# A new order table for a linear-attention and gated-MLP kernel

## The chip, the cores and the metric

The kernel runs on 1 core of one Trainium2 chip. The metric is device time of one execution in microseconds (us). The engines are PE (TensorE), DVE (VectorE), ACT (ScalarE), POOL (GpSimd) and SP (SyncE, which here only issues DMAs).

## The reference, cut to what matters

```python
# attention: 4 batches, 8 heads, 768 steps, head size 48
for t in range(S):
    state = alpha[:, :, t, :, None] * state + einsum('bhd,bhe->bhde', k[:, :, t], v[:, :, t])
    y[:, :, t] = einsum('bhd,bhde->bhe', q[:, :, t], state)
x = y.transpose(0, 2, 1, 3).reshape(B, S, H * D)          # 4 x 768 x 384
h = maximum(x @ w_in, 0)                                    # 384 -> 1024
u, v = h[..., :512], h[..., 512:]
v_n = (v - mean(v)) / sqrt(var(v) + 1e-6)                   # over the 512
v_s = einsum('ts,bsd->btd', w_spatial, v_n) + b_spatial[None, :, None]
out = (u * v_s) @ w_out                                     # 512 -> 384
```

All inputs and the output are float32; the matmuls work on bfloat16 copies.

## The kernel before, in words

**The work.** The recurrence is cut into chunks of 128 steps: 6 chunks a batch, 24 in all, numbered i = 0 to 23. Chunks 0 to 7 are done in pairs j = 0 to 3 (`pair`, even and odd steps in two halves, par 0 and 1); from chunk 8 on one at a time (`first`). A chunk goes through: load of alpha, k, q and v (`ac`, `kc`, `qc`, `vc`); logarithm (`lnp`, `ln`); its running sum as a matmul with a triangle (`cump`, `cum`); two exponentials (`einvp`, `eexpp`); scaled k and q (`ktp`, `qtp`); their transposes (`tr` for pairs, `trk` for single chunks) with copies out of PSUM (`ev`); scores (`sc`) and their mask (`m`); the state's update on PE (`updq`, `upd`) with `z`, `S` and `sb` behind it (`sb` writes the state as the right-hand matrix of the next chunk); the outputs (`ya` for both chunks of a pair, `y` for the part from the state); the copy `xs`, the transposes `xt` and their copies `xe`, which give the MLP its input.

The MLP of batch b then has: `v` (one matmul group a 128-row tile) with its statistics `bn`, `rs` and the normalised `vn`; `u`; `s` (times the spatial matrix, in two parts, mm 0 and mm 1); the product `g`; `o` and the store `st`. The weights are loaded in six pieces: `w_in` half 1, half 0, `w_sp` 0 to 2 and `w_out`, each with copies to bfloat16 (`cast`); the spatial matrix is transposed on PE (`wt`, copies `we`); `bb` and `be` spread its bias.

**The order.** The functions do not emit instructions; they record operations (`Op`) with their engines and dependences in a list. `replay` then goes through the text `PLAN` (lines 57 to 109 of the file) and emits them in that order. A word is an engine's letter (P, D, A, G for POOL, S for the issue of a DMA, Q for its landing) and the operation's number. Each engine runs its own words strictly in the order in which they stand, and an instruction that waits holds up all behind it on that engine. The framework adds the semaphores.

**Fillers.** A number behind a colon, as in `P58:512:512:192`, is a filler: `bank` (line 176) emits an fp32 matmul of so many columns on the constant `junk` (line 188) ahead of the operation, into the PSUM bank that the operation is about to use. The result is never read. Each shows as two matmul records in the trace.

**PSUM.** Eight banks are handed out in turn (`bank`), so an operation that takes a bank also waits for the readers of the bank taken eight turns earlier.

**Tiles of TensorE.** Most matmuls use the full array of 128 rows. The scores, the `trk` and `wt` transposes, the `xt` of single chunks, `ya` and most of `updq` have operands on 64 rows or fewer and use 64-row tiles (`sc` of pairs also 64 columns); `bb` has a single row and uses a 32-row tile. `updq` begins with eight 128-row matmuls (line 536) and goes on with 64-row ones (line 544).

Numbers that the text uses: 49, 51, 53, 55 are the loads of pair 0 (`ac`, `kc`, `qc`, `vc`), 109, 111, 113, 115 those of pair 1; 57 is `lnp,0`, 117 `lnp,1`, 58 `cump,0,0`, 22 `cast,w_in,1,1`, 82 `sb,0`, 96 `y,1`, 94 `xt,0`, 98 `xt,1`, 100 `v,0,0`, 92 `ya,0`, 250 `wt,2`, 259 `wt,5`, 398 `trk,8`, 369 `y,7`.

Lines: 432 and 637 issue the loads of pairs and of single chunks, 1084 those of weights, 443 is `lnp`, 452 `cump`, 502 `tr`, 574 `sc` of pairs, 601 `ya`, 614 `y` of pairs, 365 and 389 `xt`, 710 `trk`, 745 `sc` of single chunks, 831 `wt`; line 819 is the helper through which all MLP matmuls go, 198 and 200 the copies on ACT and on the other engines.

Of the kernel before, what the change touches and what calls it, by code (L numbers as in the profile page):

```python
# [63 lines left out]
G85 P193 A139 P103 D140 S324 Q325 A202 D206 G141 D196 P152 A104 D143 G142 A194 P215 S29 Q30 D105 G192 P153 A330 P157  # L64
G144 P207 D154 A106 G145 D158 P155 P331 D209 A156 D216 P341 A208 P159 G28 A332 D217 P212 A160 G210 A26 D214 P172 G211
A342 D213 P161 A333 G27 A173 D335 P218 S33 Q34 A343 A162 S328 Q329 P219 D345 P170 G334 A220 S382 Q383 D163 P223 P349
P221 A224 S384 Q385 P164 G344 D350 A222 P339 D174 A171 P225 P337 A165 P168 D340 A226 P166 D107 A175 D338 P227 A167
D176 D108 A169 P230 D32 A228 D177 P238 A231 D31 P247 S386 Q387 D35 A239 P347 D232 A248 P250 P244 A249 P242 G36 D229
A348 P236 A252 D251 P362 A233 S37 Q38 G346 D245 P253 D246 A243 G336 P240 D364 A237 S424 Q425 P351 A390 D363 A255 S428
Q429 D235 P359 A254 D234 P391 A352 D353 S388 Q389 P274 D360 A393 A241 G354 P270 A392 D356 P275 D361 A395 G394 P266  # L70
D276 P267 G357 D396 P271 A40 G39 D268 P398 D272 P259 S426 Q427 G355 A400 P365 D399 A261 D260 P256 G358 P405 S430 Q431
D366 A432 P369 P278 G269 D370 S495 Q496 P367 P433 D258 A368 P371 G273 D257 P279 S41 Q42 D407 A372 P294 A434 G397 D406
# [12 lines left out]
P679 S747 Q748 G647 D650 P721 A624 P556 G547 A723 D651 P557 A681 D722 G563 P652 D680 S783 Q784 P682 D558 A653 P686
G555 P728 D683 S877 Q878 P654 D687 P536 A656 G684 A655 P537 D688 A720 S873 Q874 G648 P786 D729 P752 A787 P564 S907
Q908 G685 D538 A754 A758 P724 P657 D730 A753 S875 Q876 G539 A789 P565 D725 A658 D790 S990 Q991 P731 G755 A756 D566
P689 A732 P568 D757 G788 A690 D659 P759 A569 P733 S879 Q880 G726 P691 P576 D734 A692 G559 D625 A735 A760 S909 Q910
P762 P736 A761 G567 D693 D577 S944 Q945 A881 P792 D763 P766 G727 A794 D793 P882 S1027 Q1028 P694 D768 A737 G791 A883
D767 P699 G764 S986 Q987 A884 A695 P795 G765 P769 A886 S950 Q951 D796 P588 A700 G885 A915 D887 S948 Q949 P584 A770  # L90
D797 A696 S946 Q947 P889 D585 P771 A738 P798 D772 P701 A773 D891 A589 D799 P774 A890 D888 S911 Q912 D739 P703 A775
D702 P800 P896 S578 Q579 A704 D801 P580 A660 D802 D898 S304 Q305 P813 A581 D897 S988 Q989 P892 A740 P803 D776 S1023
Q1024 A952 P811 A994 S913 Q914 D661 P697 A814 D742 A804 P916 D741 P572 D893 S300 Q301 A917 D662 A918 P809 D805 G919
A920 S992 Q993 P815 A698 D812 A806 P953 S312 Q313 P829 A955 A573 D808 S590 Q591 P821 D807 A954 S1025 Q1026 D921 P995
A810 P822 G956 A997 S1029 Q1030 A996 P817 A957 D823 G894 S1057 Q1058 P899 A999 P825 D816 G959 A900 P830 D1000 G824
A922 S582 Q583 P818 D958 D831 P826 G998 D819 P901 P923 P960 A903 D827 S1059 Q1060 A925 P837 D902 G828 D820 A962 P926
# [12 lines left out]
"""


# [1048 lines left out]
```

## Time and profile before

| what | value |
|---|---|
| median of 3 runs | 142.24 us (142.18 to 142.88) |
| the profiled execution | 142.43 us |
| its span | 140.6 us |
| PE busy | 135.3 us, 96% of the span |
| DVE, ACT, POOL busy | 118.5, 108.1, 83.9 us |
| mean granted TensorE clock | 0.997 |
| HBM read, written | 23.60 MB, 4.72 MB |

The span runs from the first to the last instruction that the profile shows; the rest of the time lies around it. A busy PE is not PE at its peak: matmuls overlap and their ends are modelled, so the distance from one start to the next is the better measure of what a matmul costs.

### The profile page before, as it was taken

How to read it: one execution, taken by the hardware profiler on the slowest of the kernel's cores; microseconds unless marked ns; L12 is line 12 of the kernel's file. 1: busy time of each engine (PE TensorE's matmuls, PEld its weight loads, DVE VectorE, ACT ScalarE, POOL GpSimd, SP SyncE). 2: the span in 40 equal slices, each digit the busy share in tenths (PEclk: the TensorE clock that was granted, in tenths of full speed). 3: DMA queues.
4: the chain of work that ended last, by engine and by line, in shares of the span. 5: the costliest groups of instructions: out<-in, count | busy, mean ns of one | idle time of the engine just before them, and what ended most of it. 6: DMA issues, size and time to landing. Idle time of an engine off the chain costs nothing.

```text
span 140.6 us, 4974 instructions
## 1 busy us (share of the span) xinstructions
PE 135.3 (96%) x1921; PEld 84.1 (60%) x1921; DVE 118.5 (84%) x292; ACT 108.1 (77%) x279; POOL 83.9 (60%) x148
## 2 busy tenths in 40 slices
PE   7999999999999999999999999999999999999990
PEld 3357566574767656665665765656657666566560
DVE  7187799989999789899689999999899899987850
ACT  3487898899976678999989699989967978751021
POOL 6816458861469996970289999402788599002520
PEclk9999999999999999999999999999999999999998
DMA  4999997989999979989999998999999120005535
GB/s 101 320 324 328 338 254 245 295 286 315 267 226 161 306 145 215 203 175 210 188 199 190 188 200 171 199 200 220 257 222 225 71 107 7 0 23 212 215 146 192
DMA packets 89000, 28.64 MB, mean 204 GB/s; under 512 B 83728, under 2 KB 87440, under 8 KB 88976
## 3 DMA queue, kind: packets, MB, share of 16 engines
q1 hardware_dynamic: 88944, 28.32, 81.8%
q8 instruction: 15, 0.25, 0.7%
q14 instruction: 9, 0.07, 0.2%
q0 software_dynamic: 32, 0.00, 0.0%
HBM read 23.60 MB, written 4.72 MB: 201 GB/s over the span
## 4 chain that ended last, share of the span: by engine, by line
PE 59%; ACT 9%; DMA 9%; SPq 7%; POOL 5%; DVE 5%; issue 4%; ACTq 0%; POOLq 0%
PE bank L819 42%; SPq L432 7%; DMA raw_w<-in_moe_w_in_dram 5%; DMA ac<-in_alpha_dram 3%; PE bank L710 3%; PE bank L745 2%; PE bank L773 2%; PE bank L731 2%; PE bank L657 2%; PE bank L767 1%; POOL kt L681 1%; DMA out_dram<-raw_w 1%; PE bank L389 1%; POOL kt L474 1%; ACT vn L880 1%
## 5 line engine op out<-in xcount | busy, mean ns | idle before, releaser
L819 PE MATMUL bank<-w_spT,vn 128*128 128x384 bf16 x192 | 35.9, 326 | 0.0
L980 POOL TENSOR_TENSOR gT<-vsb,uT 128x384 bf16<-128x384 f32 x27 | 25.0, 939 | 12.5 <-DVE vsb L967 12.1
L819 PEld LDWEIGHTS <-vn 128*128 128x128 bf16 x192 | 17.3, 97 | 10.2
L681 POOL TENSOR_TENSOR kt<-kc,binv 128x384 bf16<-128x384 f32 x16 | 14.6, 917 | 11.9 <-ACT bc L676 7.3
L756 DVE TENSOR_TENSOR ptm<-bank,mask 128x512 bf16<-128x512 f32 x32 | 20.5, 680 | 0.7 <-PE bank L745 0.6
L819 PE MATMUL bank<-xT,w_in 128*128 128x384 bf16 x96 | 19.9, 326 | 0.0
L967 DVE TENSOR_TENSOR vsb<-bank,bsp_bc 128x384 f32<-128x384 f32 x31 | 16.6, 551 | 3.6 <-PE bank L819 3.0
L819 PE MATMUL bank<-w_in,xT 128*128 128x512 bf16 x72 | 18.8, 379 | 0.3 <-ACT xT L198 0.2
L819 PE MATMUL bank<-w_out_sb,gT 128*128 128x384 bf16 (+1 forms) x100 | 18.6, 320 | 0.0
L198 ACT COPY kqT<-bank 128x512 bf16<-128x512 bf16 x28 | 15.9, 598 | 2.2 <-PE bank L710 1.5
L335 POOL TENSOR_TENSOR state<-state,bc 128x192 f32<-128x192 f32 x20 | 10.1, 506 | 12.4 <-DVE mvs L896 5.5
L200 POOL CAST sbd<-state 64x192 bf16<-64x192 f32 x40 | 13.7, 341 | 2.1
L204 ACT ACTIVATE v_sb<-bank 128x512 bf16<-128x512 f32 x20 | 12.0, 602 | 2.4 <-PE bank L819 2.3
L884 DVE BATCH_NORM_STATS2 stats<-v_sb 128x6 f32<-128x512 bf16 x20 | 13.6, 682 | 0.0
L204 ACT ACTIVATE uT<-bank 128x384 bf16<-128x384 f32 x23 | 10.9, 492 | 2.2 <-PE bank L819 2.0
L819 PEld LDWEIGHTS <-w_in 128*128 128x128 bf16 x96 | 8.7, 97 | 5.9
L198 ACT COPY xT<-bank 128x192 bf16<-128x192 bf16 (+1 forms) x25 | 9.0, 377 | 4.1 <-PE bank L389 2.9
L819 PEld LDWEIGHTS <-gT 128*128 128x128 bf16 x100 | 8.8, 97 | 5.0
L188 PE MATMUL bank<-junk 128*128 128x512 f32 (+6 forms) x22 | 10.7, 613 | 1.1 <-DVE junk L1050 1.1
L585 DVE TENSOR_TENSOR ptm<-bank,mask 128x512 bf16<-128x512 f32 x16 | 10.3, 682 | 1.0 <-PE bank L574 1.0
L198 ACT CAST x_sb<-bank 128x384 bf16<-128x384 f32 x19 | 9.0, 494 | 2.3 <-PE bank L773 2.3
L916 DVE TENSOR_SCALAR vn<-v_sb,mvs,rstd 128x512 bf16<-128x512 bf16 x24 | 8.9, 404 | 1.5 <-ACT rstd L909 1.5
(129 smaller groups left out, 281.2 us busy)
## 6 DMA issues: line engine op xcount, KB each, us to landing
ac<-in_alpha_dram SPq DMA_DIRECT2D x16, 192.0 KB, 4.0
kc<-in_k_dram SPq DMA_DIRECT2D x16, 192.0 KB, 4.0
qc<-in_q_dram SPq DMA_DIRECT2D x16, 192.0 KB, 4.2
vc<-in_v_dram SPq DMA_DIRECT2D x16, 192.0 KB, 4.0
raw_w<-in_moe_w_spatial_dram SPq DMA_DIRECT2D x3, 768.0 KB, 5.5
out_dram<-raw_w SPq DMA_DIRECT2D x11, 192.0 KB, 2.9
out_dram<-o_sb SPq DMA_DIRECT2D x9, 192.0 KB, 1.9
ac<-in_alpha_dram SPq DMA_DIRECT2D x4, 384.0 KB, 4.6
```

What stands on the lines that cost most here:

```text
L188: nc.tensor.matmul(out=flat[:, 0:cols].rearrange("p (a b) -> p a b", a=4), lhsT=junk, rhs=junk[:, None, 0:n].to_broadcast([128, 4, n]), st ...
L198: nc.scalar.copy(out=out, in_=in_)
L200: ENG[eng].tensor_copy(out=out, in_=in_)
L204: nc.scalar.activation(out=out, in_=in_, func=AF.Relu)
L335: ENG[eng].tensor_tensor(out=st["state"], in0=st["state"], in1=st["bc"][:, :, None].to_broadcast([128, HP, D]), op=ALU.mult)
L585: nc.vector.tensor_tensor(out=st[f"ptm{par}"][:, s], in0=st[f"pt{s}{par}"], in1=mask2[:, par], op=ALU.mult)
L681: ENG[eng].tensor_mul(out=k_blocks(kt3)[:, :, :, 0:D], in0=quad(st["kc"]), in1=st["binv"])
L756: nc.vector.tensor_tensor(out=st["ptm"][:, s], in0=st[f"pt{s}"], in1=mask4, op=ALU.mult)
L819: return lambda ps: nc.tensor.matmul(out=out(ps), lhsT=lhsT(), rhs=rhs(), start=start, stop=stop)
L884: nc.vector.bn_stats(out=stats, in_=d["v_sb"][:, tt, :])
L967: nc.vector.tensor_tensor(out=hold["vs"], in0=ps[:, 0:TH], in1=bsp_bc[:, th, :], op=ALU.add)
L980: ENG[eng].tensor_tensor(out=bt[b]["gT"][:, dsl, cols], in0=hold["vs"], in1=bt[b]["uT"][:, dsl, cols], op=ALU.mult)
```

## The change

Only the text of `PLAN` changes; every function stays as it is. The words are in another order on every engine, and 12 fillers with 4724 columns take the place of 11 with 4312. The first six lines of each:

```diff
-D0 S49 Q50 D17 D13 S109 Q110 G47 Q48 D5 S53 Q54 G10 D7 S51 Q52 D2 D3 D11 G18 D15 D12 D1 S55 Q56 A57 G14 S111 Q112 G16
-P58:512:512:192 P264 A59 P68 A60 S113 Q114 G9 A69 D62 A70 D6 P66:512:232 S115 Q116 D71 P262 A67 D4 P74 A117 D61 S178
-Q179 D72 A263 P128:492 D75 A265 P118 D73 A129 P76 S19 Q20 P64 A130 G131 D65 A119 D77 S180 Q181 A120 G63 D132
-P134:512:108 P86 G121 D122 A135 P78 D87 S182 Q183 P126 D88 P124 P89 D80 S184 Q185 A186 P136 D91 A79 A127 D90 G81 A137
-G123 D83 A125 G82 P149:512:500 A133 S322 Q323 P146 D151 P92 A22 D150 P96 A93 P197 D23 A97 D21 P94 D147 P187 A198 P98
-A95 S24 Q25 D148 G200 A188 P100:228 A189 G190 P203 S326 Q327 A199 P138 D191 A101 D201 G84 A99 P195 D102 G8 A204 P205
+D0 S109 Q110 D17 D4 S49 Q50 G47 Q48 D11 S51 Q52 D13 S53 Q54 D15 D12 G16 D3 D1 D6 D5 D2 G9 S111 Q112 G14 S113 Q114 A57
+G8 A117 P58:512:512:192 S55 Q56 P68 A59 P262 P264 A69 G61 P118 A70 S178 Q179 P128 A60 D72 G71 P64 A119 D263 A129 S115
+Q116 G18 D65 A130 D62 A120 D265 P66:512:468 S19 Q20 P76 D122 G131 P74 A77 D75 S180 Q181 D132 A63 G73 D67 G10
+P136:512:244 P86 D137 S182 Q183 P126 G121 D87 P134 P78 A127 D88 A135 S184 Q185 P89 D80 A79 P124 A133 D91 P149 G81 A186
+D90 A125 D83 P92:512 D150 S322 Q323 P146 G22 A23 D93 P187 A21 G82 P197 D148 A188 G123 D7 P96 D151 P94 G84 A95 D97 S24
+Q25 G190 A198 P100:448 D147 A199 G200 P98 A189 P138 D201 A99 D191 G85 P203 A139 A101 S326 Q327 D140 P195 P193 G141
...
```

PE's order from `v,0,4` to `y,7`, written with the operations' names (a colon shows a filler):

```
before: ... v,0,4 v,0,5 u,0,1,1 wt,1 tr,k,3,1 wt,2 wt,0 u,0,3,1 u,0,0,1 sc,3,1 wt,3 u,0,2,1 updq,3
        sc,3,0 cum,8 s... (six parts) trk,8 wt,5 ya,3 wt,4 sc,8 y,7
after:  ... v,0,4 tr,k,3,0 v,0,5 u,0,1,1 tr,k,3,1 wt,0 wt,1 wt,2:164 u,0,0,1 u,0,3,1 sc,3,1 wt,3 updq,3
        sc,3,0 u,0,2,1 s... cum,8 ... (six parts) trk,8 wt,5:512:136 ya,3 wt,4 sc,8 y,7
```

After `v,0,0`, the table before has no filler; the new one has those at `wt,2` and `wt,5`. On SP the loads begin, in their order:

```
before: ac pair 0, ac pair 1, qc 0, kc 0, vc 0, kc 1, qc 1, vc 1, ac 2, w_in half 1, kc 2, ...
after:  ac pair 1, ac pair 0, kc 0, qc 0, kc 1, qc 1, vc 0, ac 2, vc 1, w_in half 1, kc 2, ...
```

More of the change, by code (lines that the diff above doesn't have):

```diff
@@ L68 @@
[L68 to L72, printed above, removed]
@@ new lines @@
+D90 A125 D83 P92:512 D150 S322 Q323 P146 G22 A23 D93 P187 A21 G82 P197 D148 A188 G123 D7 P96 D151 P94 G84 A95 D97 S24
+Q25 G190 A198 P100:448 D147 A199 G200 P98 A189 P138 D201 A99 D191 G85 P203 A139 A101 S326 Q327 D140 P195 P193 G141
+A204 P103 A194 D143 G142 S324 Q325 P205 D102 A192 P152 G144 A202 D206 P153 A104 P157 D196 S29 Q30 P207 A330 D105 P215
+A154 P331 D209 A208 A158 D217 P155 G210 A156 P159 D216 G145 P212 A160 P341 D213 A27 G26 P172 A332 D214 G28 P161 A342
+G211 A333 S33 Q34 P218 A173 S328 Q329 D335 A343 P223 S382 Q383 D174 P219 P170 A106 S384 Q385 A162 G334 P339 D345 P168
@@ new lines @@
+A224 P166 D163 A220 G344 A169 P349 P221 D171 P225 A175 P164 D107 A222 D177 A226 P227 D176 A165 D350 A167 P337 D340
+P230 D108 A338 D31 P238 A228 D32 P347 A231 S386 Q387 G35 D229 P244 P247 A239 A348 G36 D246 P250:164 D249 P236 A252
+D251 P242 D248 A245 D232 S37 Q38 G336 A346 P362 P253 A237 P351 D363 S424 Q425 A243 A233 D364 P359 A390 S388 Q389 P240
+D234 A254 P266 D353 A352 D235 S430 Q431 A255 P391 G354 D361 P267 A393 A241 D356 P270 A392 D360 P274 A395 G394 D268
+P271 D396 P275 D272 P398 D276 S426 Q427 G39 A40 D399 A400 G355 S428 Q429 P259:512:136 P365 A261 D260 G277 P256 S495
@@ new lines @@
+Q496 A432 P405 D366 P369 P278 D258 G357 A370 S41 Q42 D406 P367 G269 A257 P279 D407 A368 P371 S461 Q462 P433 G358 D280
+A372 P373 A397 S499 Q500 G273 P376 A434 A374 S463 Q464 P282 G436 A435 D375 P401 A437 P408 A377 P294 D438 A409 P283
+D402 A439 P410 G403 P440 D284 P295 A442 D441 P443 A412 P286 D296 S497 Q498 G44 A503 P287 D281 A411 G297 A45 S465 Q466
+P290 D444 A469 D378 P447 S592 Q593 G43 P504 P291 D288 A505 G445 P422 D449 A46 S467 Q468 G404 P470 A507 D292 P418 S501
+Q502 A472 A471 D448 P413 A474 G473 D508 S594 Q595 P420 A414 D423 P298 G506 A419 D421 S596 Q597 A379 P416 D475 G293
@@ new lines @@
+P450 S598 Q599 A417 P306 A299 D451 G285 S663 Q664 A476 P477 D307 P452 P510 A479 G289 P302 D454 D478 A453 D415 A600
+G446 P484 S626 Q627 A511 P480 P601 D486 A512 P318 S705 Q706 A303 D481 D509 A603 P513 A602 G482 D485 P314 S711 Q712
+A605 G604 D515 A319 P487 S665 Q666 A315 P455 D606 G483 A488 D514 S632 Q633 P608 G607 A456 P489 P516 D490 A610 D491
+S628 Q629 P310 D609 A517 D457 A671 P615 S630 Q631 P518 A311 P611 D520 P492 A634 D519 D612 A458 D616 P521 A493 D459
+S667 Q668 P532 D617 A522 P530 A494 D460 S669 Q670 P528 D380 A523 D381 P534 S709 Q710 A713 D524 P635 A533 P672 D531
@@ new lines @@
+P540 S707 Q708 A525 P548 A535 D527 S743 Q744 A674 A637 P560 D526 A636 P541 A639 G638 S777 Q778 A529 P618 D640 P549
+A673 G613 D542 S781 Q782 P714 A619 P544 G675 A716 A676 P561 S747 Q748 A715 D677 G614 P545 A718 D550 S749 Q750 P620
+G641 P642 D562 A621 P552 G543 A622 D643 S745 Q746 A644 P645 D719 P553 A720 G717 D646 S873 Q874 P623 D546 D554 G647
+P649 S779 Q780 A624 P721 G551 P679 D651 P556 A681 D650 G678 P557 A722 G547 D723 P652 S875 Q876 A680 D558 P682 A653
+P686 G563 D683 S877 Q878 P728 A785 P654 D688 P536 A656 G555 A655 S783 Q784 D687 P537 A751 P786 A758 D730 G684 P752
@@ new lines @@
+S909 Q910 A787 P564 G648 D538 A754 P657 A789 S316 Q317 D729 G685 A753 P565 D790 A756 S879 Q880 G539 P724 A658 P731
+D566 P689 D725 G755 A732 P568 D757 A690 D625 A881 G788 P733 S907 Q908 P759 P691 P576 A760 D734 D735 G726 S986 Q987
+D693 A761 D692 P736 D659 G567 S1023 Q1024 A569 P762 A577 P792 G559 A737 S944 Q945 D763 P766 D793 P882 A794 P694 D767
+G764 A884 A883 G727 D768 P795 A738 P584 D797 A695 G885 P699 A886 D796 A585 G765 P769 D887 A696 P588 G888 D770 A791
+P889 D700 A589 P771 S1063 Q1064 P798 A890 D891 P701 D739 S911 Q912 A799 P703 D772 S948 Q949 A740 D773 D702 P800 P896
@@ new lines @@
+S913 Q914 A802 D801 P774 A660 D898 A704 P697 D742 A915 D662 S992 Q993 P811 A994 D741 P803 D897 A775 S946 Q947 A698
+P580 D776 A952 S990 Q991 P813 A581 D812 P916 A804 P953 S1025 Q1026 D661 P892 A917 P809 D805 A955 A918 S988 Q989 P995
+A920 P572 D814 A806 S950 Q951 D921 A954 P815 D808 A997 A996 P817 D893 A573 D807 P829 G894 A957 S574 Q575 P818 A999
+G922 D958 S312 Q313 A810 P830 G956 D1000 S1059 Q1060 P821 D831 S590 Q591 P822 G919 D819 S1057 Q1058 P825 D816 G832
+P899 S1027 Q1028 P826 D823 A900 P960 G824 D827 P901 P923 A961 P926 D902 D903 P837 A925 G895 D962 D924 P904 G998 D927
@@ new lines @@
+S578 Q579 P838 S1061 Q1062 A905 G928 P967 A1031 D839 P930 G1001 P1002 S308 Q309 D968 P833 G828 A1003 S1029 Q1030 D969
+P1032 A959 P845 S586 Q587 G929 A1034 D932 A1033 P846 S304 Q305 A1036 G820 D931 P963 P834 A1004 D1037 P933 G1035 D835
+P853 A934 D847 P1039 D964 A854 P935 P1009 D848 A1065 G965 P841 S855 Q856 D936 A1041 D1040 P1066 S582 Q583 G836 P849
+D1010 A937 A1067 D1011 P1005 G966 A1069 P970 A1038 P842 D1006 G1068 D1070 A850 P857 A971 D843 S851 Q852 G1007 P1072
+A858 S320 Q321 P972 P1046 G1008 A974 D973 P1012 S570 Q571 D1074 A1073 P1042 D1047 S859 Q860 P978 A1013 D1043 P1014
@@ new lines @@
+P1075 A979 D1048 G1044 P938 A1015 A1071 D1077 G1045 P975 A1016 A939 D1076 G844 P1049 A976 D906 P1078 P984 A1079 D840
+P1017 A1050 D977 A985 P1051 P1080 P865 A1052 D940 A1018 P980 D1081 A941 D1053 P982 D866 P1054 D1082 A983 D1019 P1083
+A1055 D943 P869 A1020 D981 A1084 D942 P1089 D1056 P1091 P1095 D1085 P1093 D1022 P861 A1086 D1021 A870 D1087 P1101
+D1090 P1105 D1088 P1113 D862 P1102 D1096 S863 Q864 P1097 D1092 S871 Q872 D1103 P1098 S300 Q301 P1109 G1104 S867 Q868
+D1099 P1106 P1110 G1100 D1107 P1114 D1094 G1108 P1125 D1111 P1121 D1115 P1122 D1112 P1126 D1116 D1123 P1117 P1118
@@ L109 @@
+G1124 P1136 D1119 P1128 D1127 G1120 D1137 P1132 D1129 S1138 Q1139 P1144 D1133 S1130 Q1131 P1148 S1134 Q1135 A1145
+P1140 D1149 S1146 Q1147 P1152 A1141 S1150 Q1151 D1153 S1142 Q1143 S1154 Q1155
 """
```

40 lines of the change are left out of this document (removed).

## The prediction

> **What bounds the kernel now.** I read the page's first two parts, then the chain, then three long windows.
>
> ```profile
> span 140.6 us, 4974 instructions
> PE 135.3 (96%) x1921; PEld 84.1 (60%) x1921; DVE 118.5 (84%) x292; ACT 108.1 (77%) x279; POOL 83.9 (60%) x148
> ...
> PE   7999999999999999999999999999999999999990
> ...
> GB/s 101 320 324 328 338 254 245 295 286 315 267 226 161 306 145 215 203 175 210 188 199 190 188 200 171 199 200 220 257 222 225 71 107 7 0 23 212 215 146 192
> ```
>
> The profiled run took 142.43 us, its span 140.6, so 1.83 us lie around the span. PE is busy in every slice, so only four things can move the end: PE's own work, the price of its tiling changes, its fillers (the fp32 matmuls on `junk`, L188) and the waits still left.
>
> ```profile
> 20.00:45.00 25.00, 24.22 (x504) 16.40 (x503) 23.79 (x59) 21.54 (x56) 16.28 (x33) 1.00 0.99 261
> 45.00:119.00 74.00, 73.76 (x1093) 46.26 (x1091) 66.84 (x160) 65.31 (x177) 52.49 (x87) 1.00 0.87 186
> 119.00:137.00 18.00, 18.00 (x123) 10.84 (x118) 14.42 (x34) 6.54 (x19) 4.60 (x5) 1.00 0.31 113
> ```
>
> Second column: length; third: PE busy; then weight loads, DVE, ACT, POOL. After 45 us PE idles 0.24 us in 92; between 20 and 45 us 0.78, with DVE at 23.79 of 25. The early part is a race of four engines; the rest is PE alone, and the chain of waits ends the same way:
>
> ```profile
> 119.20 15.55 PE bank L819 x93
> 134.77 0.57 DVE raw_w L200
> ...
> 135.36 1.71 DMA out_dram<-raw_w
> ```
>
> **The change, step by step.** All engines' orders are rewritten, but the matmuls are the same apart from fillers, and both orders come to one common point: `y,7` (43.86 us before, quoted below) has the same PE work ahead of it in both tables. So I price the way to `y,7`, then the rest.
>
> *Tiling changes.* The price first: `trk,8` (16 transposes on 64 rows) is followed by 64-row work, `trk,9` by 128-row work.
>
> ```profile
> 42.33 0.29 PE L710 MATMUL bank<-ident,kt 64*128 64x64 bf16 x8
> ...
> 42.57 0.34 PE L831 MATMUL bank<-ident,w_row 64*128 64x64 bf16 x12
> ...
> 43.15 0.34 PE L831 MATMUL bank<-ident,w_row 64*128 64x64 bf16 x12
> 43.53 0.40 PE L745 MATMUL bank<-kqT 48*128 48x128 bf16 x8
> 43.86 0.34 PE L614 MATMUL bank<-sbd,kqT 128*128 128x96 bf16 x4
> ```
>
> ```profile
> 48.98 0.28 PE L710 MATMUL bank<-ident,kt 64*128 64x64 bf16 x8
> ...
> 49.31 0.66 PE L819 MATMUL bank<-w_spT,vn 128*128 128x384 bf16 x3
> ```
>
> Start to start, 0.24 against 0.33 us: a change costs about 0.09 us, an excursion 0.19. Three fewer would be worth 0.55 us. But in the built instruction order I count 37 excursions from 128-row tiles before (35 to 64 rows, 2 to 32) and 37 after (36 and 1). The table counts operations: 36 runs of 64- or 32-row operations become 33. It doesn't see that `updq` begins with eight 128-row matmuls (L536), nor that fillers are 128-row matmuls. After, three fillers stand inside 64-row runs (ahead of `ya,0`, `wt,2`, `wt,5`). All changes of tile shape together go from 78 to 79, so the headline gain is about nothing. From `v,0,0` to `y,7` there are 25 in place of 23: **+0.19 us**. After `y,7` each order has 21 excursions.
>
> *Fillers.* They go from 4312 to 4724 columns.
>
> ```profile
> 1.05 4.42 PE L188 MATMUL bank<-junk 128*128 128x512 f32 x6 [1.05 <-DVE junk L1050]
> 5.27 0.52 PE L452 MATMUL bank<-la,le_pair 128*128 128x384 bf16 x1
> 5.61 0.50 PE L452 MATMUL bank<-la,lt_pair 128*128 128x384 bf16 x1
> 14.80 1.92 PE L188 MATMUL bank<-junk 128*128 128x512 f32 x4
> 16.65 0.64 PE L574 MATMUL bank<-kqT 48*64 48x128 bf16 x32
> ```
>
> The 1012 columns from 14.80 to 16.65 take 1.85 us; less the tiling change at their end, 0.09, and the start of the first, that is 1.7 ns a column. Before, no filler stands behind `v,0,0`; after, 164 columns at `wt,2` and 648 at `wt,5` do, 812 x 1.7 = **+1.38 us** of PE work that must be run. If PE would have waited there anyway, it shows as waits missing below.
>
> *Up to `v,0,0`.* After loads `ac` of pair 1 ahead of that of pair 0.
>
> ```profile
> 4.28 0.84 ACT L443 ACTIVATE la<-ac 128x768 bf16<-128x768 f32 x1 [2.26 <-DMA ac<-in_alpha_dram]
> 17.19 0.62 ACT L198 CAST w_in<-raw_w 128x512 bf16<-128x512 f32 x1 [0.34 <-DMA raw_w<-in_moe_w_in_dram]
> 16.08 0.73 POOL L200 CAST sbd<-state 64x192 bf16<-64x192 f32 x2
> 26.22 0.61 POOL L200 CAST w_in<-raw_w 128x512 bf16<-128x512 f32 x1 [0.25 <-DMA raw_w<-in_moe_w_in_dram]
> 17.73 0.34 PE L614 MATMUL bank<-sbd,kqT 128*128 128x96 bf16 x4
> ...
> 18.86 0.33 PE L365 MATMUL bank<-ident,x_sb 128*128 128x128 bf16 x3
> 19.03 0.60 PE L188 MATMUL bank<-junk 128*128 128x228 f32 x2
> 19.51 0.82 PE L819 MATMUL bank<-w_in,xT 128*128 128x512 bf16 x3
> ```
>
> `lnp,0` (the ln at 4.28) then waits for the second load. Loads leave SP about 1.2 us apart (384 KB each at the 320 GB/s of the page's early slices), so the first `cump` starts near 6.5, not 5.27. Most of that is caught up, because the next anchor is a landing: nine loads stand ahead in both orders, so `w_in` half 1 lands at about 17.17 as now. But after, POOL runs `cast,w_in,1,1` ahead of `sb,0`, and `y,1` needs `sb,0`. So POOL: 17.17 + 0.61 + 0.73 with 0.1 between, 18.6; `y,1` near 18.75 in place of 17.73, with `xt,0` and everything on PE's queue behind it. I walked PE's queue there and find it at 18.3, so it waits 0.4 us. Then `y,1` 0.18, `xt,0` 0.17 (18.86 to 19.03), the filler of 448 columns 0.76: `v,0,0` at 19.85 against 19.51, **+0.34 us**. Bounds: +0.2, were the landing 0.1 us earlier, to +0.9, see the second rival. `xt,1` now stands behind `v,0,0`: **+0.17**.
>
> *Waits from `v,0,0` to `y,7`.* Before, by starts of rows against the same operation unhindered:
>
> ```profile
> 21.20 0.85 PE L502 MATMUL bank<-ident,qt 128*128 128x128 bf16 x8
> 21.89 0.39 PE L502 MATMUL bank<-ident,kt 128*128 128x128 bf16 x4
> ...
> 23.36 0.24 PE L574 MATMUL bank<-kqT 48*64 48x128 bf16 x2
> ...
> 24.15 0.51 PE L614 MATMUL bank<-sbd,kqT 128*128 128x96 bf16 x8
> ```
>
> ```profile
> 26.37 0.42 PE L574 MATMUL bank<-kqT 48*64 48x128 bf16 x16
> 27.02 1.47 PE L819 MATMUL bank<-w_in,xT 128*128 128x512 bf16 x6 [0.24 <-ACT xT L198]
> ...
> 34.49 0.40 PE L502 MATMUL bank<-ident,kt 128*128 128x128 bf16 x4
> 35.12 0.52 PE L831 MATMUL bank<-ident,w_row 64*128 64x64 bf16 x24 [0.23 <-DVE w_row L200]
> ...
> 36.65 0.42 PE L574 MATMUL bank<-kqT 48*64 48x128 bf16 x16
> 37.00 0.35 PE L831 MATMUL bank<-ident,w_row 64*128 64x64 bf16 x12
> ```
>
> Eight transposes of 21.20 take 0.69 where 0.45 would do (four take 0.22): 0.25. `sc` takes 0.35 unhindered (36.65), 0.79 at 23.36 and 0.65 at 26.37: 0.47 and 0.33. At 34.49, 0.63 in place of 0.32: 0.31. `wt,4` at 43.15, 0.38 against 0.18: 0.20. Small ones add 0.2: 1.78 us in all. After, walking the four queues with the durations of these rows, I find about 1.25: 0.2 at `tr,q,2,0`; 0.35 at `xt,2` and `xt,3`, whose `xs` moved from DVE to ACT behind `lnp,3` (0.84); 0.1 at `y,5`, whose `sb,4` stands on POOL behind two `w_in` casts; 0.4 at `v,0,4`, whose `xe,4` is queued on ACT behind `rs,0,2`, which waits for two statistics on DVE (behind it wait `xe,5`, `u,0,0,0` and so the casts' DVE work); 0.2 small. At `wt,5` I find none: its cast on ACT ends near 42.5, before PE arrives, so the filler there covers nothing. Bounds 0.3 (none but the anchors) to 1.8 (as now). Net **-0.53 us**.
>
> *After `y,7`.* Same work, same changes; the windows leave 0.24 us of idle PE to win, and the other engines stand further ahead of a late PE. Bounds -0.75 (ends are modelled, so idle is understated) to +0.9; I take **-0.1**. The tail from the last matmul to the store keeps its steps.
>
> Sum: 0.34 + 0.17 + 1.38 + 0.19 - 0.53 - 0.1 = +1.45; 142.43 + 1.45 = 143.88, say **143.9 us**. The median of the runs shown is 142.24, 0.19 below the profiled run; I keep the profiled run's basis.
>
> **Rivals.** *Every wait goes (not slower).* The fillers may stand where PE must wait anyway, and a PE that arrives later finds everything ready: no waits from `v,0,0` to `y,7` in place of 1.78, and 0.75 won behind it. Then 0.34 + 0.17 + 1.38 + 0.19 - 1.78 - 0.75 = -0.45: 142.0 us. For it: fillers before end within tenths of their release, as at 19.51. Against: the ACT and POOL queues above. It decides where the waits left after fall below 0.5 us with that later gain whole. 0.10.
>
> *The clock comes late.* The windows give a granted 1.00, yet 384 columns take 0.34 us at 5.27 (0.167 each in the chain's 93), and the first 1216 filler columns 4.22 us, 3.5 ns each; by 14.80 the speed has doubled. After, PE idles from 5.27 to about 6.5, which may restart the count. At half speed `cump`, `bb` and `tr,k,0,0` end 1.2 us later; `y,1` then waits for PE, not for POOL, and `v,0,0` comes near 20.4: +0.5 us, 144.4. 0.28. The Trainium skill (TensorE: Matmul & The Clock Gate, Part 1) says that the clock is judged in free-running windows of about 3.4 us, so that the same kernel warms up sooner or later from run to run. By that rule this case comes and goes between runs; the trace's half-speed steps in the first 5 us agree with it, and no row here shows what a gap does.
>
> *A new wait behind `y,7`.* One store (`st,0,4`) now stands early among the loads on SP, and loads of late chunks (`vc,23`) ahead of earlier ones. One late load starves PE by about its 1 us: 144.9. Against: loads land ahead of use now. 0.12.
>
> **How the numbers follow.** The forecast has 0.45, the rivals 0.10, 0.28 and 0.12, the rest 0.05. The range runs from 142.7 (half of the first rival left out) to 145.2 (the last one and some). A measurement of this kernel tells about 0.5% (0.7 us) from no change: against 142.24, faster ends at 141.5 and slower begins at 142.95. Faster needs more than every wait gone: 0.03. Same, the first rival and a sliver of the forecast: 0.12. Slower: 0.85.
>
> **What would show it.** After: the first `cump` near 6.5; `y,1` near 18.7 with PE waiting on POOL's `sbd`; `v,0,0` 19.8 to 20.4; `y,7` 45.1 to 45.8; from there to the end 93.2 us as now; 79 tiling changes at 0.09. I am wrong if `y,7` comes before 44.5, or if PE's idle after it is over 1 us.

## The result, and the profile after

The changed kernel takes 145.74 us (median of 6 runs, 145.64 to 147.36) against 142.21 us, a ratio of 1.027 (95% interval 1.021 to 1.0329); the ratio of the medians is 1.025. The forecast was 143.9 us with a range to 145.2; the direction was right, the size less than half of what came. The profiled run took 145.75 us with a span of 144.0, against 142.43 and 140.6: 3.3 us more. Single runs of both kernels and of several below lie 1.5 to 3 us higher; where a trace caught one, the TensorE clock was granted late or halved for a stretch, and the ratios below leave most of them out, while the 1.027 holds two near 147.3 us.

The page of the kernel after, first lines:

```profile
span 144.0 us, 4965 instructions
PE 135.6 (94%) x1923; PEld 84.2 (58%) x1923; DVE 119.9 (83%) x297; ACT 106.6 (74%) x275; POOL 84.4 (59%) x147
...
PE   7699979799999999999999999999999999999990
```

PE is busy 0.3 us longer than before, the span 3.3 us longer: PE idles more. Of its 40 slices of 3.6 us the sixth (18.0 to 21.6) and the eighth (25.2 to 28.8) fall to 7, in tenths busy; before, all slices but the first and the last stand at 9. What PE waited for (us in total, times, longest):

```profile
PE bank L452 <- ACT la L443: 1.4, 1, 1.4
...
PE bank L574 <- issue: 1.0, 1, 1.0
PE bank L614 <- POOL sbd L200: 1.0, 1, 1.0
```

The kernel before has none of the three. They are, with the anchors of the prediction, in PE's timeline (start, length, and in brackets the idle time ahead and what ended it):

```profile
6.42 0.32 PE L452 MATMUL bank<-la,le_pair 128*128 128x384 bf16 x1 [1.39 <-ACT la L443]
...
19.07 0.33 PE L614 MATMUL bank<-sbd,kqT 128*128 128x96 bf16 x4 [0.96 <-POOL sbd L200]
...
20.21 0.81 PE L819 MATMUL bank<-w_in,xT 128*128 128x512 bf16 x3
...
25.15 0.41 PE L574 MATMUL bank<-kqT 48*64 48x128 bf16 x15
26.57 0.24 PE L574 MATMUL bank<-kqT 48*64 48x128 bf16 x1 [1.01 <-issue]
...
36.57 0.55 PE L188 MATMUL bank<-junk 128*128 128x164 f32 x2
...
44.30 1.36 PE L188 MATMUL bank<-junk 128*128 128x512 f32 x4
...
46.67 0.34 PE L614 MATMUL bank<-sbd,kqT 128*128 128x96 bf16 x4
```

The first `cump` is where it was forecast (6.42, about 6.5). `y,1` waits for POOL's `sbd` as said, but starts at 19.07, not 18.75; `v,0,0` at 20.21, not 19.85. The two fillers behind it are there. New is the row at 26.57: 15 of the 16 matmuls of `sc,2,1` run, and PE idles 1.01 us ahead of the last with "issue" as the reason, which means that nothing the profile follows held it. `y,7` comes at 46.67, 2.81 us later than before, and from there to the end of the span it is 97.31 us against 96.79.

Windows show the same (length; PE, weight loads, DVE, ACT, POOL busy; then the granted clock, the DMA engines' share and GB/s): first the kernel before from `v,0,0` to `y,7` and behind, then the kernel after.

```profile
19.51:43.86 24.35, 23.57 (x491) 15.73 (x490) 23.27 (x57) 21.56 (x56) 15.73 (x31) 1.00 0.98 263
43.86:118.20 74.34, 74.10 (x1093) 46.79 (x1091) 67.08 (x160) 64.94 (x177) 52.73 (x87) 1.00 0.88 188
```

```profile
20.21:46.67 26.46, 25.24 (x499) 16.78 (x499) 22.41 (x54) 22.88 (x59) 15.46 (x28) 1.00 0.96 251
46.67:121.00 74.33, 73.97 (x1092) 46.52 (x1089) 66.21 (x159) 65.27 (x177) 50.97 (x84) 1.00 0.89 195
```

Ahead of `y,7` PE's work has grown by 1.67 us (the fillers) and its idle time from 0.78 to 1.22; behind, idle went from 0.24 to 0.36, and since ends are modelled, that is less than the way shows.

In the form of the prediction: `v,0,0` +0.70 (forecast +0.34), from there to `y,7` +2.11 (0.17 + 1.38 + 0.19 - 0.53 = +1.21), behind `y,7` +0.52 (-0.1).

### The profile page after: what moved, and what is told of

The parts are those of the page before. It is cut to its first block, busy times and chain, and to the rows that moved or that the text cites. A ratio compares the mean times of both kernels' runs of the same rounds, so it can differ in the third digit from the quotient of the medians.

```text
span 144.0 us, 4965 instructions
## 1 busy us (share of the span) xinstructions
PE 135.6 (94%) x1923; PEld 84.2 (58%) x1923; DVE 119.9 (83%) x297; ACT 106.6 (74%) x275; POOL 84.4 (59%) x147
## 4 chain that ended last, share of the span: by engine, by line
PE 65%; POOL 13%; SPq 7%; DMA 5%; ACT 4%; issue 3%; DVE 2%; POOLq 0%
PE bank L819 45%; SPq L432 7%; POOL gT L980 6%; DMA raw_w<-in_moe_w_in_dram 5%; POOL sbd L200 3%; PE bank L710 2%; PE bank L745 2%; PE bank L188 2%; POOL state L335 2%; PE bank L657 2%; PE bank L773 2%; PE bank L767 1%; PE bank L731 1%; PE bank L389 1%; PE bank L544 1%
## 5 line engine op out<-in xcount | busy, mean ns | idle before, releaser
L819 PE MATMUL bank<-w_spT,vn 128*128 128x384 bf16 x192 | 36.0, 326 | 0.0
L980 POOL TENSOR_TENSOR gT<-vsb,uT 128x384 bf16<-128x384 f32 x26 | 23.8, 925 | 14.0 <-DVE vsb L967 13.5
L819 PEld LDWEIGHTS <-vn 128*128 128x128 bf16 x192 | 17.1, 97 | 10.5 <-DVE vn L916 0.3
L819 PE MATMUL bank<-xT,w_in 128*128 128x384 bf16 x96 | 19.1, 326 | 0.0
L819 PE MATMUL bank<-w_out_sb,gT 128*128 128x384 bf16 (+1 forms) x100 | 18.8, 320 | 0.1
L819 PE MATMUL bank<-w_in,xT 128*128 128x512 bf16 x72 | 18.7, 379 | 0.2 <-ACT xT L198 0.2
L198 ACT COPY raw_w<-bank 128x384 f32<-128x384 f32 x9 | 4.3, 494 | 11.1 <-PE bank L819 11.1
L188 PE MATMUL bank<-junk 128*128 128x512 f32 (+6 forms) x24 | 11.3, 593 | 1.1 <-DVE junk L1050 1.1
L819 PEld LDWEIGHTS <-w_in 128*128 128x128 bf16 x96 | 8.7, 97 | 5.6 <-issue 0.2
L819 PEld LDWEIGHTS <-gT 128*128 128x128 bf16 x100 | 8.7, 97 | 5.4 <-POOL gT L980 0.2
L819 PEld LDWEIGHTS <-xT 128*128 128x128 bf16 x72 | 6.3, 97 | 6.6 <-ACT xT L198 1.5
L691 DVE TENSOR_TENSOR qt<-qc,bank 128x384 bf16<-128x384 f32 x16 | 8.7, 546 | 1.5 <-ACT bank L686 1.5
```

Source lines behind the costliest of these rows:

```text
L188: nc.tensor.matmul(out=flat[:, 0:cols].rearrange("p (a b) -> p a b", a=4), lhsT=junk, rhs=junk[:, None, 0:n].to_broadcast([128, 4, n]), st ...
L198: nc.scalar.copy(out=out, in_=in_)
L819: return lambda ps: nc.tensor.matmul(out=out(ps), lhsT=lhsT(), rhs=rhs(), start=start, stop=stop)
L980: ENG[eng].tensor_tensor(out=bt[b]["gT"][:, dsl, cols], in0=hold["vs"], in1=bt[b]["uT"][:, dsl, cols], op=ALU.mult)
```

## The experiments

The first theory was the prediction's: the fillers cover nothing and cost 1.4 us and their changes, `y,1`'s wait is on the path, and something unforeseen holds `sc,2,1`. The rivals: PE would wait there anyhow; the early part is set by landings; or `sc,2,1` waits for data. The letter says what was edited: a_ the changed kernel, b_ the one before, h_ half of each, c_ several edits at once. Each trace is of a single execution.

This table has the way in each trace, us, from the rows of `v,0,0` (L819), `y,7` (L614) and the end of the span:

| kernel | v,0,0 at | to y,7 | y,7 to end |
|---|---|---|---|
| before | 19.51 | 24.35 | 96.79 |
| after | 20.21 | 26.46 | 97.31 |
| after_again | 18.98 | 27.35 | 97.26 |
| a_both | 19.06 | 25.89, 1.6 of it from a halved clock | 97.26 |
| a_pad30 | 19.89 | 26.15 | 97.27 |
| b_late | 20.03 | 23.84 | 97.62 |
| b_fill | 19.23 | 25.55 | 96.81 |
| h_before_after | 19.75 | 24.59 | 97.41 |
| h_after_before | 22.43, clock late | 26.16 | 96.88 |

### The fillers and GpSimd's cast: a_nofill, a_cast, a_both

```diff
-P250:164 ... P259:512:136          a_nofill
+P250 ... P259
-P146 G22 A23 D93 P187 A21 G82      a_cast
+P146 A23 D93 P187 A21 G82 G22
```

> The changed kernel without the two words of filler matmuls at wt,2 and wt,5 (812 columns an operation pair, 3912 columns with what their words hold). Theory: they cover no wait, so the whole price goes: 1.38 us of columns and about four tiling changes, 0.38 us; about 144.0 us, 1.2 to 1.8 us under the changed kernel on the same chip. Rival: they stand where TensorE would wait for the weights' transposes anyhow; then the waits take their place and the time falls by less than 0.4 us.

> The changed kernel with GpSimd's cast of the second half of w_in moved back behind GpSimd's sb,0. Theory: y,1 no longer waits 1.13 us for sb,0, v,0,0 starts about 1.0 us earlier than its 20.21 us, and the end comes 0.7 to 1.1 us earlier. Rival: v,0,0 is paced by the landing of w_in's second half and by the other engines' shares of the cast; then y,1 is early, v,0,0 moves by less than 0.3 us and the end by less than 0.3 us.

> Both edits in the changed kernel: no fillers at wt,2 and wt,5, and GpSimd's cast behind its sb,0. Theory: the two gains lie one behind the other on TensorE's path and add, about 143.0 us (2.2 to 2.8 us under the changed kernel). Rival: what is won at one place is waited for at the next (wt or tr operations that are not ready); then the gain is no more than the larger of the two alone.

a_both: 1.0074 of the time before (1.0022 to 1.0126), 1.1 us over it in place of 3.1 to 3.8 (1.0216 in after_again, 1.027 above). a_cast: 1.0249 (1.0161 to 1.0338), no gain that can be told. a_nofill's times give no ratio, but the traces do: from the first `wt` matmul to `y,7` it takes 9.02 us, a_both too (35.93 to 44.95), the kernel after 10.55 (36.12 to 46.67), all at full clock. So the two fillers cost **1.53 us** there, against 1.57 forecast with their changes.

With the cast moved (a_cast), `y,1` stands at 17.80 in place of 19.07 and `v,0,0` 1.26 us earlier, as expected, yet `y,7` only 0.09 earlier. The wait inside `sc,2,1` did not take it back: it keeps its length (1.02 us) and ends 1.25 us earlier, at 25.32. The clock did: a_both's page and timeline,

```profile
PEclk9999999779999999999999999999999999999999
```

```profile
27.22 2.77 PE L819 MATMUL bank<-w_in,xT 128*128 128x512 bf16 x6
```

where in a_pad30 (below) the same six matmuls take 1.46 us. PEclk is the granted clock in tenths, in 40 slices: for 3.4 us from 26.57 it was halved, which cost 1.31 us there and 0.28 at the `cump` ahead, 1.6 in all. a_cast and a_nofill show the same. So a_cast doesn't tell what `y,1`'s wait is worth at the end: `v,0,0` moved, against the rival, and what was won was lost to the clock.

### What the wait inside sc,2,1 is: a_rows, a_pad30, c_pad14, b_late

The suspicion came from the DMA queues: q8, "instruction", moves 0.25 MB in 15 packets, 16 KB each, and the trace after has 3846 records of PE and its weight loads: about 256 a packet. The DMA view, cut to windows, of the kernel before (20.8 to 22.7 us) and of the kernel after (18.3 to 24.2, then 24.2 to 25.2); columns are packets, MB and the share of 16 engines' time:

```profile
q1 hardware_dynamic: 503, 0.35, 63.7%
q8 instruction: 1, 0.02, 6.0%
```

```profile
q1 hardware_dynamic: 2807, 1.68, 101.2%
```

```profile
q1 hardware_dynamic: 740, 0.30, 107.0%
q8 instruction: 1, 0.02, 5.8%
```

Before, the second packet comes at 20.81 us in a lull of the bulk loads. After, loads fill all 16 engines up to 24.2, the packet comes at 24.25 to 25.17, and PE goes on at 26.57, 1.4 us behind it, with 702 of its records done. In a_cast, a_both and a_nofill the wait also ends 1.3 to 1.5 us behind the packet's landing, with 702 records done, at 25.32, 25.17 and 29.05 us. To tell a fetch from data, instructions are put ahead of it that change nothing else:

```diff
-P58:512:512:192                    a_rows
+P58:512:512:16:16:16:16:16:16:16:16:16:16:16:16
-        for cols in fill:          a_pad30, with P58:512:512:192:-30; c_pad14: a_both with :-14
+        for cols in (c for c in fill if c > 0 or [nc.tensor.ldweights(junk.bitcast(BF16)[:, 0:2]) for _ in range(-c)] is None):
-P100:228                           b_late, in the kernel before
+P100:512:228
```

> The changed kernel with its first word of fillers cut into more, shorter matmuls: the same columns, 11 more instructions ahead of everything in TensorE's program. It tells what the 1.25 us wait inside sc,2,1 is (the 16th matmul's weights are held from 25.35 to 26.57 us). Theory, the fetch of TensorE's own instructions: the wait stays at the same place of the instruction stream and so shows about 11 instructions earlier, ahead of about the 10th matmul of sc,2,1, of like length. Rival, a wait for data or for a bank: it stays ahead of the 16th matmul. End within 0.4 us of the changed kernel in both cases.

> The changed kernel with 30 loads of two columns of weights, which nothing uses, put into TensorE's program behind the first fillers, where it waits for its first data: the same work in the same order, 30 instructions later in the program. Theory, the wait inside sc,2,1 is for the fetch of TensorE's own instructions (16 KB each; in the three runs that have the wait it ends 1.3 to 1.5 us after the landing of the second fetch, ahead of the same program row): the wait moves 30 rows earlier in the work, to about the first matmul of sc,2,1 or ahead of it, and is shorter or gone, as the fetch is asked for earlier; end 0.3 to 1.2 us earlier. Rival, a wait for data, a bank or the array: it stays ahead of the 16th matmul of sc,2,1 with 1.0 to 1.3 us.

> Both edits of a_both (no fillers at wt,2 and wt,5, GpSimd's cast behind its sb,0) with 14 such weight loads ahead. Theory of the fetch: the 0.8 us wait inside sc,2,1 moves to another place or goes, and where no window of TensorE's work is thin the clock isn't halved behind it (3.4 us at half clock, some 1.6 us): 141.3 to 142.6 us, at or under the kernel before. Rival (data): as a_both, 143.3 to 144.0 us with the wait at its old place.

> The kernel before with one filler of 512 columns more ahead of v,0,0 (0.87 us of TensorE). Theory: the second fetch of instructions, which in the kernel before starts at 20.81 us, is asked for 0.9 us later and stands behind the loads qc,6 and kc,6 (issued 20.16 and 20.64 us); TensorE waits for it about 1 us at program row 680, and the end is 1.3 to 2.2 us later, more where the clock is halved behind it. Rival, the fetch has nothing to do with it: no such wait, and the end is 0.3 to 0.9 us later, since waits of 0.24 and 0.45 us that follow in the kernel before are absorbed.

a_rows doesn't decide: each small filler loads its own fp32 weights, the first `cump` comes at 9.61, the clock at 16.66, `y,1` 5 us later than in the changed kernel (24.22). The packet lands before PE needs it, and no wait shows. c_pad14 decides:

```profile
27.19 0.31 PE L574 MATMUL bank<-kqT 48*64 48x128 bf16 x8
28.34 0.31 PE L574 MATMUL bank<-kqT 48*64 48x128 bf16 x8 [0.84 <-issue]
```

Fourteen instructions more ahead, that is seven pairs of weight load and matmul, and the wait stands seven matmuls earlier: 8 and 8 in place of 15 and 1. It again ends 1.3 us behind the packet's landing, with 702 records done. This trace has the clock at 13.74 us only and `v,0,0` at 22.25, but that isn't what moves the wait: a_nofill, as late (22.15), has it ahead of the 16th matmul. No data dependence moves so. It is **the fetch of PE's own instructions**. That the packet is late because the bulk loads fill the engines fits the windows above, but no run varied the loads alone, and when the packet is asked for doesn't show. In after_again, from 20.0 to 21.0 us, the engines are half empty,

```profile
q1 hardware_dynamic: 249, 0.15, 52.4%
```

and the packet still comes at 23.46 only. (c_pad14's time, 1.0021, 0.9977 to 1.0066, is the kernel before's within the interval; its lowest runs, 142.7 to 142.8 us, are just over what was expected.) With 30, in a_pad30, the packet comes at 21.1 and the wait is gone. But look what stands behind it:

```profile
24.82 0.42 PE L574 MATMUL bank<-kqT 48*64 48x128 bf16 x16
...
25.72 0.34 PE L365 MATMUL bank<-ident,x_sb 128*128 128x128 bf16 x3
26.82 0.34 PE L365 MATMUL bank<-ident,x_sb 128*128 128x128 bf16 x3 [0.76 <-ACT x_sb L198]
```

`xt,3` now waits for `xs,3` on ACT, behind `lnp,3`, as the prediction named it, with 0.76 us. From `v,0,0` to `y,7` only 0.31 us are won, and the time, 1.0174 (1.0119 to 1.0228), is not distinct from the changed kernel's. The fetch hid a wait for data.

b_late went against its theory: no fetch wait (the packet, at 22.63, was still in time) and no loss, ratio 1.0006 (0.9975 to 1.0037). The filler put `v,0,0` at 20.03, and 23.84 us later `y,7` at 43.87, as in the kernel before (43.86): half a microsecond of PE's lateness is absorbed there, since waits for others stand behind it. Behind `y,7` its trace is 0.83 us longer than the kernel before's, by one wait that the kernel before does not have:

```profile
87.14 0.32 PE L657 MATMUL bank<-la,ut_ones 128*128 128x384 bf16 x1 [0.84 <-ACT la L651]
```

### Which part of the table: h_before_after, h_after_before, b_fill

The h_ kernels take one table's words up to `y,7` (P369) and the rest in the other's order.

> The table of the kernel before up to y,7 and from there all that is left in the changed kernel's order, engine by engine. Theory: the difference of 3.3 us between the kernels lies ahead of y,7 but for about 0.6 us; so within 0.6 us of the kernel before. Rival: the late part of the changed table is the dear one or needs its own early part: 1 us or more over the kernel before.

> The changed table up to y,7, and from there the order of the kernel before. Theory: the late order of the kernel before is worth 0.5 us whatever runs ahead of it: 96.8 us from y,7 to the end, and 0.3 to 0.8 us under the changed kernel. Rival: a late TensorE gives its engines no such gain, or the seam costs: 97.3 us or more from y,7 to the end.

```diff
-P250 ... P259                      b_fill, in the kernel before
+P250:164 ... P259:512:136
```

> The kernel before with the changed kernel's fillers at wt,2 (164 columns) and wt,5 (512 and 136). Theory: they cover nothing there; 812 columns at 1.7 ns are 1.38 us, and with the four changes of tiling 1.4 to 1.9 us on the way from wt,1 to y,7 (8.74 us in the kernel before) and 1.2 to 1.9 us in the time. Rival: they take the place of waits (0.20 us at wt,4) and of work that other engines then catch up: under 0.7 us.

Behind `y,7` the two traces take 97.41 and 96.88 us, each as the kernel whose order it has there: the changed order is 0.5 us the dearer, as both theories say. It is so whatever runs ahead: all eleven traces with it take 97.26 to 97.41. The old order is not as steady: 96.79 to 96.88 in three traces (before, b_fill, h_after_before), but 97.62 in b_late and 97.36, 97.39 and 97.61 in c_back, c_sum and c_sumpad (below), each with a wait that the three don't have, so what runs ahead can cost it all of its advantage. h_before_after's time, 1.0069 (1.0031 to 1.0108), is 1.0 us over the kernel before: more than its theory's 0.6, just short of its rival's 1, with both in the interval; in its trace half of that stands ahead of `y,7`, where its order is the old one. h_after_before gives no ratio (its trace has the clock granted at 14 us only). b_fill: the time 1.0107 (1.007 to 1.0145), 1.5 us more as expected; the way from `v,0,0` to `y,7` 1.20 us longer, a little less than expected, because 0.3 us at `tr,k,3,1` and 0.2 at `wt,4`, waits of the kernel before, go at the same time.

### The other early edits: a_ac, a_padxs

```diff
-D0 S109 Q110 D17 D4 S49 Q50        a_ac: ac,0 loaded first
+D0 S49 Q50 D17 D4 S109 Q110
-A330 D105 P215 A154 P331 D209 A208 A158      a_padxs: a_pad30, and xs,2 and xs,3 on DVE
+A330 D105 D154 D158 P215 P331 D209 A208
```

> The changed kernel with its first two loads in the order of the kernel before (ac,0 ahead of ac,2), nothing else. Theory: the first cump comes near 5.3 us again in place of 6.42, so TensorE is not idle between its fillers and its first work; y,1 and v,0,0 are set by the landing of w_in and by GpSimd, so the best time stays within 0.4 us of the changed kernel's 145.7; but the clock, which in runs of the changed kernel and its variants came as late as 13 us or was halved again, is granted by 8 us in each run and the spread between runs falls. Rival: the early part is on the path to the end; the best time falls by 0.8 us or more.

> a_pad30 (30 unused weight loads ahead) with xs,2 and xs,3 back on VectorE, as in the kernel before. In a_pad30 the wait inside sc,2,1 was gone, but xt,2 then waited 0.76 us for ScalarE's xs,3 behind lnp,3. Theory: this second wait was hidden behind the first and goes too; from v,0,0 to y,7 the way is 0.5 to 0.9 us shorter than a_pad30's 26.1 us. Rival: it goes over into the next wait (cump,3,0 or v,0,3), less than 0.3 us shorter.

a_ac: `cump` at 5.56, `y,1` at 18.68 still waiting 0.95 us for POOL; 1.012 (1.0074 to 1.0165), some 1.4 us better than the changed kernel's 1.0216 (after_again, measured on another chip), so the rival (early part on the path) holds there. Its own trace has the fetch wait and a halved clock, so it can't show where the gain lies: left open. The spread did not vanish. a_padxs went the rival's way: `xt` waits 0.19 us, but then `y,5`, with its `sb,4` on POOL:

```profile
31.65 0.50 PE L614 MATMUL bank<-sbd,kqT 128*128 128x96 bf16 x8 [0.68 <-POOL sbd L200]
```

From `y,1` to `y,7` it takes 27.65 us, a_pad30 27.29. One wait gives way to the next: ACT's, then POOL's. (One execution only, so there is no ratio.)

### The price of an excursion: b_inside, b_between

```diff
-P440 ... P452 ... P484             b_inside: 20 words inside 64-row runs behind y,7
+P440:4 ... P452:4 ... P484:4
-P373 ... P413 ... P416             b_between: 20 words between 128-row operations behind y,7
+P373:4 ... P413:4 ... P416:4
```

> The kernel before with 20 fillers of 4 columns inside runs of 64-row tiles behind y,7: each opens an excursion into 128-row tiles more (118 changes of tiling in place of 78). Theory: beside the filler itself, an excursion costs two changes of 0.095 us, so 3 to 4.6 us over b_between in the way from y,7 to the end. Rival: the changes lie beside the other engines' work, under 1 us over b_between.

> The kernel before with the same 20 fillers between operations on 128-row tiles behind y,7: no change of tiling more. It carries the price of the fillers alone, which is to be taken off b_inside: 20 times 0.05 to 0.2 us on the way from y,7 to the end.

```profile
43.62 0.34 PE L614 MATMUL bank<-sbd,kqT 128*128 128x96 bf16 x4
```

```profile
span 148.2 us, 5039 instructions
```

```profile
43.67 0.34 PE L614 MATMUL bank<-sbd,kqT 128*128 128x96 bf16 x4
```

```profile
span 143.2 us, 5039 instructions
```

The first two are `y,7` and the span of b_inside, the others of b_between. From `y,7` to the end 104.6 and 99.5 us: 5.06 us for 20 excursions, **0.25 us each**, a little over the 0.19 of the prediction, and nothing hides it. (One trace each; by the 0.8 us that this order varies behind `y,7`, an estimate of the error is 0.04 each.) So excursions are worth counting; the change just has none fewer.

### Undone together: c_sum, c_sumpad, c_back; and once more: after_again

c_sum: the edits of a_both, a_ac and a_padxs (without its pads), and the order of the kernel before from `y,7`; c_sumpad: the same with `:-20`. c_back: a_both with `:-30` and the late order of before.

> All causes undone together: the changed table with ac,0 loaded first, GpSimd's cast behind sb,0, xs,2 and xs,3 on VectorE, no fillers at wt,2 and wt,5, and from y,7 on the order of the kernel before. Theory: the parts add (y,1 near 17.8, y,7 near 43.5 with the fetch wait of 0.8 to 1.3 us still there): 141.6 to 143.0 us. Rival: a cause is missing, and it stays over 143.3 us.

> c_sum with 20 unused weight loads ahead, which move the second fetch. Theory: no wait for instructions inside sc,2,1, y,7 at 43.2 or before, 141.0 to 142.3 us, at or under the kernel before. Rival: the wait is only exchanged for one on data, as in a_pad30: no faster than c_sum.

> The changed kernel, unchanged, once more. Theory: the trace shows the same parts (y,1 0.8 to 1.2 us late for GpSimd, about 1 us of wait for instructions inside sc,2,1 ahead of the 16th matmul, 10.5 us from wt,1 to y,7, 97.3 us from y,7 to the end), and the fastest runs lie at 145.4 to 146.0 us. Rival: the first chip's 145.7 was a slow case; the fastest runs here lie near 144.0 us, as those of a_ac, a_pad30 and h_after_before did, and the fetch wait is absent in them.

> The changed table without the fillers at wt,2 and wt,5, GpSimd's cast behind sb,0, 30 unused weight loads ahead, and from y,7 on the order of the kernel before. Theory: what was lost is all undone, 141.8 to 142.7 us in its fastest runs, as the kernel before, and slower ones by 1.6 us or more where the clock comes late. Rival: something that was not found keeps it over 143.0 us in its fastest runs too.

c_sum 1.012 (1.0077 to 1.0164) and c_sumpad 1.0069 (1.0042 to 1.0096): neither is as fast as hoped, with 0.7 us of new wait for POOL's `sbd` in both. c_back 1.0056 (1.0031 to 1.008), 0.8 us over the kernel before: its lowest runs, 142.85 to 142.95 us, lie between what the theory (142.7) and the rival (143.0) allow. In its trace 0.5 of that stands at one place behind `y,7`, where the kernel before waits for nothing:

```profile
49.19 0.36 PE L773 MATMUL bank<-vb,ptm 128*128 128x48 bf16 x8 [0.34 <-DVE qt L691]
```

So an order that is cheaper by itself can lose that at the seam to another: c_pad14, which keeps the changed order behind `y,7`, is as fast within the intervals (1.0021). Beside it, the loss is found but for some 0.3 to 0.8 us. No version beats the kernel before. after_again, 1.0216 (1.0171 to 1.026), has the changed kernel's time within the intervals, but not the same waits:

```profile
17.84 0.33 PE L614 MATMUL bank<-sbd,kqT 128*128 128x96 bf16 x4
...
18.98 0.81 PE L819 MATMUL bank<-w_in,xT 128*128 128x512 bf16 x3
...
25.89 0.24 PE L574 MATMUL bank<-kqT 48*64 48x128 bf16 x1 [1.56 <-issue]
```

`y,1` waits for nothing here (its loads landed earlier) and `v,0,0` is 1.23 us earlier; the fetch wait is 0.55 us longer, and `y,7`, at 46.33, only 0.34 earlier. Of what is gained ahead of the fetch, nearly half is waited for at the fetch, and about a quarter is left at `y,7`.

## Why the prediction was wrong, point by point

- **Tiling changes: right.** The traces have the 37 excursions and the 78 and 79 changes that were counted, so there is no gain; the price was somewhat higher (0.25 us each) than said.
- **Fillers: right.** 1.38 + 0.19 = 1.57 us; 1.53 measured. They cover nothing.
- **Up to `v,0,0`: right in mechanism, short in size, and not additive.** +0.34 said, +0.70 in the profiled run, because `w_in` half 1 landed at 17.56 and not at 17.17; in after_again, where it landed at 16.05, it was -0.53. POOL's cast shows both, first in the kernel after, then in after_again:

```profile
17.61 0.61 POOL L200 CAST w_in<-raw_w 128x512 bf16<-128x512 f32 x1 [2.13 <-DMA raw_w<-in_moe_w_in_dram]
18.29 0.73 POOL L200 CAST sbd<-state 64x192 bf16<-64x192 f32 x2
```

```profile
16.11 0.61 POOL L200 CAST w_in<-raw_w 128x512 bf16<-128x512 f32 x1 [0.74 <-DMA raw_w<-in_moe_w_in_dram]
16.78 0.73 POOL L200 CAST sbd<-state 64x192 bf16<-64x192 f32 x2
```

  Most of what is won or lost here is paid back further on (after_again, b_late), so a sum over stretches was the wrong form for this part.
- **Waits from `v,0,0` to `y,7`, "I find about 1.25 ... Net -0.53": the step that failed.** The way grew by 2.11 us; less the fillers' 1.53 and `xt,1`'s 0.17 there remains +0.41. So the new order waits more than the old, not less: a fetch wait of 1.0 us inside `sc,2,1` that no view of before shows, and under it waits of almost that size that I had found but priced too low: 0.35 at `xt,2` and `xt,3` (0.76 in one row of a_pad30), 0.1 at `y,5` (0.68 in a_padxs). Error: 0.9 us. (The waits of before were also summed a little high: by the rows shown, the two at `sc` are 0.44 and 0.30 us, not 0.47 and 0.33.)
- **Behind `y,7`, -0.1: wrong in sign.** +0.52, which goes with the order (both h_ kernels). "The other engines stand further ahead of a late PE" is no argument: PE's order and theirs are new too, and their order sets the waits. Error: 0.6 us. About as much stands near 85 us in the kernel after:

```profile
84.38 0.36 PE L731 MATMUL bank<-vb,kt 128*128 128x48 bf16 x8
84.85 0.33 PE L767 MATMUL bank<-sbd,kqT 128*128 128x96 bf16 x4
...
85.39 0.36 PE L773 MATMUL bank<-vb,ptm 128*128 128x48 bf16 x8
85.84 0.82 PE L819 MATMUL bank<-w_out_sb,gT 128*128 128x384 bf16 x4
```

```profile
83.29 1.50 POOL L200 CAST sbd<-state 64x192 bf16<-64x192 f32 x4
84.88 0.91 POOL L980 TENSOR_TENSOR gT<-vsb,uT 128x384 bf16<-128x384 f32 x1
```

  `upd,15` takes 0.47 us and `y,14`'s second half 0.45 to the next start, where 0.2 would do; the one is followed by `y,15`, which needs POOL's `sb,14`, the other by `o`, which needs POOL's `g`. POOL ends its casts of `sbd` at 84.79 and its `gT` at 85.79 us, 0.06 and 0.05 us ahead of PE's next starts (84.85, 85.84). So the trace puts both waits down to POOL; no run removed them.
- **Rival "the clock comes late": not in the profiled run** (granted at 4.4 us, before 6.8). But the clock was halved near 27 to 30 us in five of the fourteen traces that begin with the changed order, in a_nofill, a_cast, a_both, a_ac and c_back, and in none of the six that begin with the old one. **"Every wait goes"** is refuted by the 1.53; **"a new wait behind `y,7`"** came, as small waits for POOL, not as a late load.

The errors add: 0.36 + 0.94 + 0.62 = 1.92; 143.9 + 1.9 = 145.8.

Open: what makes the packet of instructions late; what decides whether the clock is halved; the rest of the 0.8 us by which c_back is over the kernel before; where a_ac gains.

## What to carry to other kernels

When a table of orders is rewritten, price the waits of the new order engine by engine, and let the range assume that the old order's waits are replaced, not removed: here the fetch, ACT's `xs` and POOL's `sb` lay one under another, and taking away the uppermost won 0.3 of 1.0 us. "issue" in the list of waits, on an engine with a long unrolled program, may be the engine's own code still to be fetched; a few instructions put ahead show it, since the wait moves with the count. Count excursions into small tiles in the built instruction order, fillers and mixed operations included, not in the table.

## What the runs showed of the hardware

- PE's instructions come in packets of 16 KB, about 256 of its records each: the second one of the trace came at 20.8, 21.1, 24.2 and 26.1 us in before, a_pad30, after and c_pad14. Where PE waited for it (after, c_pad14 and others), it went on 1.3 to 1.5 us behind the landing.
- The clock was halved for 3.4 us soon behind waits of 0.8 to 1.6 us at 25 to 29 us, in five kernels (a_nofill, a_cast, a_both, a_ac, c_back). The Trainium skill (TensorE: Matmul & The Clock Gate, HAM oscillation) gives as the rule that idle gaps over about 3.4 us are what to avoid; here, in a_both, the halving came behind a wait of only 0.76 us. Yet after_again, with a wait of 1.56 us, kept its clock: not settled.
- Leaving a run of 64-row work for one small 128-row matmul and coming back cost 0.25 us, from 20 of them (b_inside against b_between).
